# Plain copies out of PSUM for the first chunk's transposed blocks, and a new order of the work, in an adaLN block with sliding-window attention and a gated MLP

## The chip, the cores and the metric

The kernel runs on one core of one Trainium2 chip. The metric is the time of one execution on the device in microseconds (us), lower is better. A kernel's time is the median of its runs; a profile is one execution, with a time of its own. Engines are named as the profile names them: PE is TensorE's matmuls and PEld its weight loads, DVE VectorE, ACT ScalarE, POOL GpSimd, SP SyncE, which issues nearly all transfers.

## What is computed

The input x has one batch of 2048 rows of 640 columns in bf16. A vector c of 640 gives, through w_mod, six rows of 640: shift, scale and gate for the attention (sa, ca, ga) and for the MLP (sb, cb, gb). Both halves normalise x without learned weights, modulate it, and add their gated result.

```python
def _A_ref(x, wqkv, wo):                    # 32 heads of 20, window 256
    q, k, v = ...                           # x @ wqkv
    scores = jnp.einsum('bhqd,bhkd->bhqk', q, k) * Dh ** (-0.5)
    mask = (idx[:, None] - idx[None, :] >= 0) & (idx[:, None] - idx[None, :] < W)
    p = _softmax(jnp.where(mask[None, None], scores, -1000000000.0), axis=-1)
    o = jnp.einsum('bhqk,bhkd->bhqd', p, v)
    return o.transpose(0, 2, 1, 3).reshape(B, S, D) @ wo
...
mod = (_silu(c) @ w_mod)                    # sa, ca, ga, sb, cb, gb
h = _layernorm(x, axis=-1) * (1 + ca) + sa
x = x + ga * _A_ref(h, A_wqkv, A_wo)
h = _layernorm(x, axis=-1) * (1 + cb) + sb
x = x + gb * ((_sigmoid(h @ w_gate) * (h @ w_up)) @ w_down)
```

## The kernel before

**Tiling.** The 2048 rows are cut into eight chunks of 256 rows, each of two blocks of 128. The functions record operations, 2126 in all, for eight chunks that overlap in time: while chunk a is in its attention, chunk a+1 or a+2 is being projected and chunk a−1 is in the MLP.

**A chunk's path.** `ln1` normalises the two blocks of x (statistics on VectorE at L766 and L768, the power −1/2 on GpSimd at L771 and L773, the normalised rows at L786). The result is turned, columns onto partitions, into a tile hT of five blocks (dt 0 to 4) of 128 columns by 256 rows, and modulated with mA, which holds the shift and the scale of the attention. For chunks 0 to 2 TensorE turns it (`pe_transposes`), for later chunks a DMA transpose (L793) does, and `modulate` then works in place in SBUF (L801 on ScalarE, L802 on VectorE or GpSimd). `qkv` multiplies hT with wqkv in pieces of 320 columns (chunk 0) or 480 (the others), and ScalarE (L870) or VectorE (L871) empties PSUM into staging buffers stg, of which there are four, and V. From stg q and k are turned to QT and KT, by TensorE for chunks 0 and 1 and by DMA transposes (L793) for the rest. A score group (matmuls at L680, S<-QT,KT) is followed by exponentials on ScalarE (L981) and masks on GpSimd (L1006); a burst of matmuls multiplies with V (M<-E,V). VectorE turns the result back (T, L1050), divides (L1055, L1057) and turns again (On, L1059); On goes to DRAM and returns as oT. `outproj` multiplies with wo and adds the residual (L1111); the second normalisation and modulation give h2T; `mlp` multiplies with the gate and up weights wg and wu, takes a tanh (L1156) and a product (L1158) to hh, multiplies with wd and adds (L1177).

**The head.** Everything waits for mA: w_mod's first part comes in five slices of 320 KB, and the function fnA adds one group of ten matmuls for each slice; a copy at L752 takes mA out of PSUM. For chunk 0 the five turned blocks lie in PSUM by then, each 128 x 256, and leave it by ten operations of 128 x 128 that modulate on the way (L834 on ScalarE, L835 on VectorE): first the rows of block 0 for all dt, then those of block 1, so that the projection of block 0 can start after five. `mod_rows` makes the other modulation rows in the same manner from the parts of w_mod that are loaded into wu and hh; the scales for wo and wd are multiplied into these weights (L1200, L1139).

**What sets the order.** PRIO, a list at L360, holds one number for each recorded operation: sorting by it gives the order of the program, and the number modulo 5 gives the engine. `schedule` goes through the operations in this order and keeps times of its own estimation, which serve one purpose in the kernel: where a tile has a choice of several buffers, it gets the one that is free earliest by these times. `emit` writes each engine's instructions in that order with the semaphore waits that the data and the buffers need. Thus nothing is reordered on the chip: an instruction that waits holds up all those behind it on its engine, and on SyncE a transfer that waits for its data holds up the transfers behind it. DSAFE (L479) is a time that is added to the estimated end of every load and every DMA transpose (L576, L609, L794). It makes no instruction and no wait; it can change which buffer a tile gets.

Of the kernel before, what the change touches and what calls it, by code (L numbers as in the profile page):

```python
# [7 lines left out]
ACT = mybir.ActivationFunctionType  # L8
# [334 lines left out]
def c_act(n):  # L343
    return 0.17 + n / 1200.0


def c_dve(n, x=1.0):
    return 0.155 + n / 960.0 / x
# [6 lines left out]
def c_pe(n):  # L355
# [117 lines left out]
]  # L473
TR1 = 2
NPH = 3
NPQ = 2
PQ = ()
KEEP = 3
DSAFE = 1.5  # L479
RING = 256  # L480
FETCH = 3.3
START = 0.8
PORTLAG = 0.05
MIXED = 0.39
NPB = 0
# [18 lines left out]
def build(nc, A_x, A_wqkv, A_wo, B_x, B_w_gate, B_w_up, B_w_down, c, w_mod, out, S=2048):  # L504
    NCH = S // CH
    P = Prog(nc)
    A = P.op
# [745 lines left out]
```

## Time and profile before

| | us |
|---|---|
| median of three runs | 328.51 |
| lowest and highest of them | 326.97, 329.53 |
| the profiled execution | 330.57 |
| its span | 328.8 |
| TensorE busy (matmuls) | 320.3 |
| VectorE, ScalarE, GpSimd busy | 211.2, 214.1, 186.3 |
| mean granted clock of TensorE | 0.995 of full speed |

The profiled execution's time is that of the whole launch, 1.77 us longer than the span, which goes from the first instruction in the trace to the last. It lies 2.06 us above the median. The rows of the profile that matter stand in the prediction. In a row of a group the numbers after the bar are busy time, mean ns of one, and the idle time just before it with what ended it; in a row of a timeline they are the start, the length, the engine, the line, the operation, what it writes and reads, the shape and the count, and in brackets the wait.

### The profile page before, as it was taken

What the parts mean: (1) busy time and instruction counts of PE and PEld (TensorE: products, weight loads), DVE (VectorE), ACT (ScalarE), POOL (GpSimd) and SP (SyncE); (2) the same over time, 40 slices, a digit from 0 to 9 for tenths busy, and PEclk for the clock granted to TensorE, in tenths of its full rate; (3) what the DMA queues carried; (4) which work ended last, traced back from release to release, by engine and by line L of the source; (5) the groups of instructions that cost most, each with busy time, mean ns of one, the idle gap of its engine ahead of it and who ended that gap; (6) DMA issues with size and microseconds to landing.
All of it is one profiled execution on the core that took longest, in us unless ns stands there. A gap on an engine that the chain in (4) does not pass through costs nothing.

```text
span 328.8 us, 11616 instructions
## 1 busy us (share of the span) xinstructions
PE 320.3 (97%) x4879; PEld 223.9 (68%) x4879; DVE 211.2 (64%) x419; ACT 214.1 (65%) x317; POOL 186.3 (57%) x273
## 2 busy tenths in 40 slices
PE   8999999989999999999999999999999999999996
PEld 3664545536876568766786567877786778787885
DVE  3689996767599755684576576639463776274242
ACT  2497987868976598888687756886786762112220
POOL 6019769945968586769475848384949392002000
PEclk9999999979999999999999999999999999999999
DMA  7989897999590344932034745330602021302001
GB/s 244 371 287 375 127 238 161 182 226 248 178 166 1 67 117 60 162 62 74 22 70 84 143 72 129 66 87 24 102 3 82 23 57 28 102 20 63 20 22 40
DMA packets 71038, 37.85 MB, mean 115 GB/s; under 512 B 45258, under 2 KB 69066, under 8 KB 70986
## 3 DMA queue, kind: packets, MB, share of 16 engines
q1 hardware_dynamic: 69536, 35.47, 46.8%
q10 hardware_dynamic: 1450, 1.64, 1.9%
q8 instruction: 38, 0.62, 0.8%
q14 instruction: 14, 0.11, 0.2%
HBM read 21.30 MB, written 5.25 MB: 81 GB/s over the span
## 4 chain that ended last, share of the span: by engine, by line
PE 68%; DVE 2%; POOL 1%; issue 0%; ACT 0%; DVEq 0%
PE M L679 58%; PE S L680 6%; PE M L680 5%; POOL E L1006 1%; DVE wd L1139 1%; DVE hh L1158 1%; DVE x L786 0%; DVE hT L802 0%; DVE T L1050 0%; ACT E L981 0%; ACT sig L1156 0%; DVE x L1177 0%; DVEq L328 0%
## 5 line engine op out<-in xcount | busy, mean ns | idle before, releaser
L1006 POOL TENSOR_SCALAR_AFFINE_SELECT E<-E 128x512 bf16<-128x512 bf16 (+1 forms) x176 | 142.9, 836 | 73.0 <-ACT E L981 68.7
L981 ACT ACTIVATE E<-S 128x512 bf16<-128x512 f32 (+2 forms) x184 | 151.0, 879 | 41.7 <-PE S L680 39.6
L679 PE MATMUL M<-wqkv,hT 128*128 128x480 bf16 (+1 forms) x340 | 73.6, 361 | 2.5 <-DMA QT<-stg 1.6
L679 PE MATMUL M<-h2T,wu 128*128 128x256 bf16 x480 | 65.3, 273 | 0.0
L679 PE MATMUL M<-h2T,wg 128*128 128x256 bf16 x480 | 63.8, 273 | 1.0 <-DVE hh L1158 0.6
L1158 DVE SCALAR_TENSOR_TENSOR hh<-sig,M 128x512 bf16<-128x512 f32 x48 | 32.1, 679 | 39.8 <-ACT sig L1156 24.6
L679 PE MATMUL M<-wd,hh 128*128 128x320 bf16 (+2 forms) x396 | 56.9, 296 | 0.7 <-POOL E L1006 0.6
L1156 ACT ACTIVATE sig<-M 128x512 f32<-128x512 f32 x48 | 28.8, 605 | 42.5 <-PE M L679 37.5
L679 PEld LDWEIGHTS M<-wqkv,hT 128*128 128x128 bf16 x340 | 31.1, 99 | 31.0 <-issue 2.4
L679 PEld LDWEIGHTS M<-h2T,wg 128*128 128x128 bf16 x480 | 46.3, 98 | 8.3 <-DVE hh L1158 0.8
L679 PEld LDWEIGHTS M<-h2T,wu 128*128 128x128 bf16 x480 | 44.5, 98 | 7.8 <-issue 0.3
L679 PEld LDWEIGHTS M<-wd,hh 128*128 128x128 bf16 x396 | 37.1, 98 | 15.3 <-POOL E L1006 0.7
L680 PEld LDWEIGHTS S<-QT,KT 20*64 20x64 bf16 (+1 forms) x1856 | 19.9, 101 | 20.1 <-ACT E L981 9.2
L680 PE MATMUL S<-QT,KT 20*64 20x256 bf16 (+5 forms) x1856 | 32.1, 228 | 0.1
L1177 DVE TENSOR_TENSOR x<-M,x 128x320 bf16<-128x320 f32 (+2 forms) x33 | 15.3, 474 | 26.3 <-PE M L679 26.2
L766 DVE BATCH_NORM_STATS2 st<-x 128x6 f32<-128x320 bf16 x64 | 28.3, 478 | 3.0 <-DMA x<-in_A_x_dram 2.5
L1050 DVE STREAM_TRANSPOSE T<-M 128x512 f32<-128x512 f32 x32 | 21.1, 693 | 10.3 <-PE M L680 10.1
L679 PE MATMUL M<-wo,oT 128*128 128x320 bf16 x160 | 24.7, 300 | 0.0
L771 POOL TENSOR_SCALAR st<-st 128x2 f32<-128x2 f32 x16 | 3.6, 228 | 34.8 <-DVE st L768 34.5
L680 PE MATMUL M<-E,V 128*32 128x128 bf16 (+1 forms) x960 | 22.7, 247 | 0.0
L786 DVE TENSOR_SCALAR x<-x,st 128x640 bf16<-128x640 bf16 x26 | 14.1, 566 | 12.6 <-POOL st L773 12.6
L680 PEld LDWEIGHTS M<-E,V 128*32 128x32 bf16 x960 | 19.1, 97 | 4.3 <-issue 1.9
(74 smaller groups left out, 249.9 us busy)
## 6 DMA issues: line engine op xcount, KB each, us to landing
x<-in_A_x_dram SPq DMA_DIRECT2D x23, 160.0 KB
doc<-On SPq DMA_DIRECT2D x64, 40.0 KB
wd<-in_B_w_down_dram SPq DMA_DIRECT2D x4, 480.0 KB
wd<-in_w_mod_dram SPq DMA_DIRECT2D x5, 320.0 KB
wqkv<-in_A_wqkv_dram SPq DMA_DIRECT2D x4, 400.0 KB
wu<-in_w_mod_dram SPq DMA_DIRECT2D x5, 320.0 KB, 4.6
oT<-doc SPq DMA_DIRECT2D x8, 192.0 KB, 3.4
hh<-in_w_mod_dram SPq DMA_DIRECT2D x2, 640.0 KB
```

The lines of the kernel that those rows point to most:

```text
L679: return e.matmul(o, l, r, start=st, stop=sp, skip_group_check=True)
L680: return e.matmul(o, l, r, start=st, stop=sp, tile_position=tp, skip_group_check=True)
L766: A("dve", lambda e, g, bi=bi, j=j: e.bn_stats(v(bi * 12 + j * 6, 6), src[bi].ap[:, j * 320:(j + 1) * 320]), 0.48, reads=[src[bi].r()], wr ...
L771: A("pool", lambda e, g: e.tensor_scalar(v(28, n), var(), EPS, None, op0=ALU.add), 0.2, reads=[st.r(("m", bi)) for bi in range(n)], writes ...
L786: return e.tensor_scalar(dst[bi].ap[:], src[bi].ap[:], v(24 + 2 * bi, 1), v(30 + bi, 1), op0=ALU.subtract, op1=ALU.mult)
L981: A("act", lambda e, eng: e.activation(dst(), src(), ACT.Exp, scale=SM_SCALE), c_act(n), reads=[Sp.r()], writes=[E.r(key)], prio=3, tag=f" ...
L1006: A("pool", lambda e, eng: e.affine_select(rows(dst), rows(src), pattern=[[0, 8], [sign, n]], compare_op=ALU.is_ge, fill=0.0, base=base, c ...
L1050: A("dve", lambda e, g, h=h: e.transpose(T1.ap[:, 512 * h:512 * h + 512], X[h].ap), 0.694, reads=[X[h].r()], writes=[T1.r(h)], prio=3.5, t ...
L1139: A(WSE[1], lambda e, g, t=t: e.tensor_tensor(wd[:, t, :], wd[:, t, :], gbc[:], op=ALU.mult), WS, port=True, reads=[R_wd[t // 3], R_gbc], ...
L1156: A("act", lambda e, g, pg=pg, sg=sg: e.activation(sg.ap[:], pg.ap[:], ACT.Tanh, scale=0.5), c_act(512), reads=[pg.r()], writes=[sg.r()], ...
L1158: A("dve", lambda e, g, pu=pu, sg=sg, f0=f0: e.scalar_tensor_tensor(out=hh.ap[:, f0:f0 + 2, :], in0=sg.ap[:].rearrange("p (a b) -> p a b", ...
L1177: A("dve", lambda e, g, ps=ps, bi=bi, c0=c0, n=n: e.tensor_tensor(x1[bi].ap[:, c0:c0 + n], ps.ap[:, 0:n], x1[bi].ap[:, c0:c0 + n], op=ALU. ...
```

## The change

There are three parts.

1. In chunk 0 the five turned blocks leave PSUM by five plain copies of 128 x 256, which need no mA. `modulate` then works on them in place in SBUF, one operation for each dt, and each waits for the copy of its own dt and for mA. That is ten operations where there were ten. TensorE's transposes for chunks 1 and 2 are as they were.
2. DSAFE goes from 1.5 to 0.3.
3. PRIO is replaced as a whole: both the order and the engine of the 2126 operations. The matmuls are the same ones in another order. Of the five copies four are on ScalarE (dt 1, 0, 3, 4) and one on VectorE (dt 2); of their five modulations four are on VectorE (dt 1, 0, 2, 4) and one on ScalarE (dt 3). In TensorE's order three of the five transposes of chunk 0 come ahead of the last two groups of fnA, where all five came after them. Of the modulations in the MLP's half, 19 are on ScalarE where 12 were, and 11 on GpSimd where 17 were.

```diff
@@ -358,125 +358,125 @@
 PRIO = [
-    153, 158, 283, 203, 1133, 1238, 163, 53, 678, 98, 103, 128, 142, 308, 208, 8, 146, 4, 136, 19, 44, 64, 69, 74, 79,
...
+    138, 143, 233, 128, 653, 33, 1593, 183, 573, 398, 38, 243, 318, 112, 163, 578, 151, 49, 166, 54, 59, 64, 69, 74,
...
-DSAFE = 1.5
+DSAFE = 0.3
@@ -793,14 +793,14 @@
-    def modulate(dst, sc, sh, Rmod, prio, ln, a):
+    def modulate(dst, sc, sh, Rmod, prio, ln, a, turned_by=None):
         for dt in range(NDT):
             def mo(e, g, dt=dt):
                 ap = dst.ap[:, dt, :]
                 if g == "act":
                     return e.activation(ap, ap, ACT.Identity, scale=sc[:, dt:dt + 1], bias=sh[:, dt:dt + 1])
                 return e.tensor_scalar(ap, ap, sc[:, dt:dt + 1], sh[:, dt:dt + 1], op0=ALU.mult, op1=ALU.add)
-            A(MOE, mo, {"dve": 0.34, "act": 0.59, "pool": 0.55}, port=True, reads=[dst.r(("t", bi)) for bi in range(2)] + Rmod,
+            A(MOE, mo, {"dve": 0.34, "act": 0.59, "pool": 0.55}, port=True, reads=[dst.r(k) for k in (turned_by or (lambda dt: (("t", 0), ("t", 1))))(dt)] + Rmod,
@@ -825,15 +825,22 @@
+        if a == 0:
+            for dt, pv, rp in evs:
+                def cp(e, g, dt=dt, pv=pv):
+                    return e.activation(dst.ap[:, dt, :], pv(), ACT.Copy) if g == "act" else e.tensor_copy(dst.ap[:, dt, :], pv())
+                A(("act", "dve"), cp, {"act": c_act(256), "dve": c_dve(256)}, reads=[rp], writes=[dst.r(("t", dt))], prio=1, tag=f"{ln}turn{a}")
+            modulate(dst, sc, sh, Rmod, prio, ln, a, lambda dt: (("t", dt),))
+            return last
         prev = {}
-        for blocks, (dt, pv, rp) in [((bi,), x) for bi in range(2) for x in evs] if a == 0 else [((0, 1), x) for x in evs]:
+        for blocks, (dt, pv, rp) in [((0, 1), x) for x in evs]:
             lo, hi = blocks[0] * 128, blocks[-1] * 128 + 128
...
-            prev[dt] = [A(("act", "dve"), ev, {"act": 0.56, "dve": 0.53} if a else {"act": 0.44, "dve": 0.40}, reads=[rp] + Rmod,
+            prev[dt] = [A(("act", "dve"), ev, {"act": 0.56, "dve": 0.53}, reads=[rp] + Rmod,
```

The numbers in braces are the planner's estimates of durations, in us.

222 rows, old and new, of the table PRIO are left out of this document.

## Prediction

> **What bounds the kernel now.** I read the busy shares first, then the rows of granted clock and of DMA rate over the span's 40 slices (8.22 us each), then what TensorE waited for.
>
> ```profile
> PE 320.3 (97%) x4879; PEld 223.9 (68%) x4879; DVE 211.2 (64%) x419; ACT 214.1 (65%) x317; POOL 186.3 (57%) x273
> ...
> PEclk9999999979999999999999999999999999999999
> ...
> GB/s 244 371 287 375 127 238 161 182 226 248 178 166 1 67 117 60 162 62 74 22 70 84 143 72 129 66 87 24 102 3 82 23 57 28 102 20 63 20 22 40
> ```
>
> TensorE is busy for 97% of the span; the other engines stand near 65%. It idles 328.8 − 320.3 = 8.5 us, so only two things can move the end: that idle time, and the slice in which the clock drops (the ninth, 66 to 74 us). The matmuls themselves are the same before and after.
>
> ```profile
> PE M L679 <- DMA QT<-stg: 1.6, 1, 1.6
> PE S L659 <- DVE E L654: 1.3, 1, 1.3
> PE M L679 <- DVE hT L835: 0.6, 1, 0.6
> PE M L679 <- POOL E L1006: 0.6, 1, 0.6
> PE M L679 <- DVE hh L1158: 0.6, 1, 0.6
> PE M L679 <- DVE T L1050: 0.5, 1, 0.5
> PE M L679 <- ACT hT L801: 0.3, 1, 0.3
> PE M L679 <- DVE V L871: 0.3, 1, 0.3
> ```
>
> The columns are total us, times, longest. 1.3 is the start of the program, which nothing here touches. The largest of the rest is one wait for a staging buffer, and it lies in the slice of the low clock. TensorE's timeline and the windows of that place:
>
> ```profile
> 61.99 1.94 PE L679 MATMUL M<-wo,oT 128*128 128x320 bf16 x13
> ...
> 65.23 0.98 PE L679 MATMUL M<-wqkv,hT 128*128 128x480 bf16 x4 [0.34 <-ACT hT L801]
> 67.81 4.07 PE L679 MATMUL M<-wqkv,hT 128*128 128x480 bf16 x11 [1.59 <-DMA QT<-stg]
> 71.81 0.43 PE L680 MATMUL S<-QT,KT 20*64 20x256 bf16 x24
> ...
> 77.59 2.20 PE L679 MATMUL M<-wqkv,hT 128*128 128x480 bf16 x10
> 79.63 1.25 PE L679 MATMUL M<-h2T,wg 128*128 128x256 bf16 x10
> ```
>
> ```profile
> 68.00:70.00 2.00, 2.00 (x7) 0.85 (x6) 1.93 (x3) 0.32 (x1) 1.82 (x3) 0.54 1.03 245
> 70.00:72.00 2.00, 2.00 (x22) 0.65 (x27) 1.97 (x3) 0.82 (x2) 0.00 (x0) 0.61 0.98 335
> ```
>
> Two waits, 0.34 and 1.59, are followed by 11 matmuls that take 71.81 − 67.81 = 4.00 us, at a granted clock of 0.54 and 0.61 (the column ahead of the last two). Undisturbed, ten of the same shape take 79.63 − 77.59 = 2.04, or 0.204 each: 11 cost 2.24. So the clock took 1.76 more, and the place cost 0.34 + 1.59 + 1.76 = 3.69 us, the largest sum in the span that an order can touch.
>
> **A: the head.** Ten evictions with modulation give way to five copies and five modulations.
>
> ```profile
> 9.88 0.35 PEld L679 LDWEIGHTS S<-silubc,wd 128*128 128x128 bf16 x10 [0.32 <-DMA wd<-in_w_mod_dram]
> ...
> 10.19 0.39 PE L679 MATMUL M<-ident,x 128*128 128x128 bf16 x4
> 10.39 0.17 DVE L752 COPY mA<-S 128x10 f32<-128x10 f32 x1 [1.63 <-PE S L679]
> ...
> 10.67 1.53 DVE L835 TENSOR_SCALAR hT<-M,mA 128x128 bf16<-128x128 f32 x4
> ...
> 11.71 2.20 PE L679 MATMUL M<-wqkv,hT 128*128 128x320 bf16 x15 [0.58 <-DVE hT L835]
> ...
> 15.67 0.23 POOL L771 TENSOR_SCALAR st<-st 128x2 f32<-128x2 f32 x1 [7.44 <-DVE st L768]
> ```
>
> ```profile
> L870 ACT ACTIVATE V<-M 128x160 bf16<-128x160 f32 x4 | 1.2, 309 | 0.1
> ```
>
> ```profile
> L802 DVE TENSOR_SCALAR h2T<-h2T,scB,shB x11: 335/345/794, 78.7 to 302.9; 128x256 bf16<-128x256 bf16 x11
> L802 DVE TENSOR_SCALAR hT<-hT,mA x5: 250/685/822, 42.0 to 145.1; 128x256 bf16<-128x256 bf16 x5
> ```
>
> The modulation's factors mA exist from 10.39 + 0.17 = 10.56; the first projection starts at 11.71, after 0.58 of waiting for the evictions. In the new order three of the five transposes stand ahead of the last two groups of the factors' matmuls, where TensorE waited 0.32 for a slice of w_mod, so their copies (some 0.31 to 0.43 each: the 160-column copy takes 0.309) are done before mA. Then four modulations on VectorE at 0.25 to 0.35 start at 10.56 instead of evictions at 1.53/4 = 0.38 a half block: the first projection matmul can go near 11.3, 0.4 earlier. But the two last transposes still come after mA, and one block (dt 3) takes copy, copy and then 0.6 on ScalarE, to about 12.1, so 0.2 of the wait returns. Taken: **−0.2**, range −0.5 to +0.4. The same VectorE form shows 0.250 at its shortest and 0.822 at its longest; were all four at 0.82, the head would cost 4 × (0.82 − 0.25) = 2.3 us. I take the short end, since GpSimd, the one engine that starts late here, had been idle 7.44 us at 15.67.
>
> The Trainium skill ("SBUF — State Buffer", section "Who interferes with whom") says that VectorE and GpSimd share one pair of SBUF ports as an exclusive lock, so that the later of the two blocks. That speaks against taking modulation from PSUM into SBUF; the spread of 250 to 822 ns agrees with it, and by it the sum would be +2.1 if GpSimd were at work there.
>
> **B: 28 to 41 us.** Two 320 KB slices of w_mod now stand last in the queue of early loads, behind wo, the gate weights and the others; before, they stood in the middle. The matmuls that need them ran at
>
> ```profile
> 32.83 0.86 PE L680 MATMUL M<-wu,silubc 128*32 128x320 bf16 x20
> ```
>
> and are set back by 16 score matmuls, five wide projection matmuls and ten transposes, some 1.9 us: needed near 34.6. The loads run at 375 GB/s in the fourth slice (to 32.9 us) and 127 in the fifth; if all of the fifth's 127 × 8.22 = 1044 KB belonged to them at 375, they would end 2.8 us into it, at 35.7; if little does, at 33. A wait of 0 to 1.1. Taken: **+0.4**, range −0.3 (small waits of this stretch hide behind it) to +1.1.
>
> **C: 64 to 72 us.** Why did the staging buffer come late? SyncE's issues (issue time, its length):
>
> ```profile
> 54.69 0.47 SPq L581 DMA_DIRECT2D wd<-in_B_w_down_dram  x1
> ...
> 62.93 1.25 SPq L793 DMA_TRANSPOSE QT<-stg  x1
> ```
>
> The DMA transpose that empties the buffer is issued at 62.93 and waited for until 67.81, 4.9 us, behind a 480 KB load. In the new order no bulk load stands between the score work of 40 us and the transposes of chunk 3 (that load goes out near 36 us, the next ones behind the transposes), and the PE work between the last write of the buffer and its next use grows from 5.3 to 7.5 us for the transpose waited for, while the other one's falls from 7.8 to 6.5 (counted through both orders at undisturbed durations like those above). Both exceed the 4.9. So the stall goes: **−1.93**. Of the clock's 1.76 I credit half, **−0.9**: the run that was profiled took 330.57, 2.06 over the median, and I can't see that the median run lost the whole of it. Something comes in place of it:
>
> ```profile
> L801 ACT ACTIVATE hT<-hT,mA 128x256 bf16<-128x256 bf16 x15 | 8.7, 601 | 0.0
> ```
>
> ```profile
> 62.16 1.94 ACT L981 ACTIVATE E<-S 128x512 bf16<-128x512 f32 x2 [0.80 <-PE S L680]
> ```
>
> First, four modulations of chunk 4 now follow each other on ScalarE behind two exponentials, 1.94 + 4 × 8.7/15 = 4.3 us after the score group, while TensorE has ten wo matmuls (10 × 1.94/13 = 1.5), five of 0.204, a score group of 0.4 and three matmuls of the first chain (0.6), 3.5 in all, before the last modulated block: **+0.7**. Second, the MLP of chunk 0:
>
> ```profile
> L1050 DVE STREAM_TRANSPOSE T<-M 128x512 f32<-128x512 f32 x32 | 21.1, 693 | 10.3 <-PE M L680 10.1
> ...
> L1059 DVE STREAM_TRANSPOSE On<-Tn 128x1024 bf16<-128x1024 bf16 x16 | 19.8, 1237 | 0.2
> ...
> L871 DVE CAST stg<-M 128x480 bf16<-128x480 f32 x14 | 9.1, 647 | 4.8 <-PE M L679 4.7
> ```
>
> ```profile
> 66.64 0.28 DVE L768 BATCH_NORM_AGGREGATE st<-st 128x2 f32<-128x12 f32 x2
> ...
> 69.92 0.81 DVE L1057 TENSOR_TENSOR Tn<-T,Dr 128x640 bf16<-128x640 f32 x1
> ```
>
> Between the P·V burst of chunk 1 and its first gate matmuls TensorE has 20 wide projections (4.1) and two score groups (0.8), 4.9; VectorE has two T transposes (1.39), an On transpose (1.24), two casts (1.29), aggregation (0.3) and four modulations (1.4), 5.6, with up to 0.8 of a divide left over ahead of them. Gate matmuls take the blocks one by one, which gives 0.4 back. Before, no wait stands at 79.63, because VectorE caught up during the stall. Taken: **+1.1**, range 0.5 to 1.9. Sum of C: −1.93 − 0.9 + 0.7 + 1.1 = **−1.0**, range −3.7 to +0.9.
>
> **D: after 80 us.** The wait of 0.5 for T goes, as the transposes of PSUM are placed ahead of the scaling of wd
>
> ```profile
> L1139 DVE TENSOR_TENSOR wd<-wd,gbc 128x640 bf16<-128x640 bf16 x9 | 6.2, 722 | 0.0
> ```
>
> and the one of 0.6 for GpSimd's mask becomes one of about 0.4 (0 to 1.5), since a residual add now stands behind two such scalings, a divide and an On transpose on VectorE. The 0.6 for hh at the end of the span goes to 0.1, its modulation being on ScalarE. Together −0.5 − 0.2 − 0.5 = −1.2; a wholly new order of some 2,100 operations also makes waits that I can't see one by one, and I put half of it back: **−0.6**, range −1.2 to +2.
>
> **Sum.** −0.2 + 0.4 − 1.0 − 0.6 = −1.4. Against the profiled execution, 330.57 − 1.4 = 329.2; on the scale of the median, 328.51 − 1.4 = **327.1**.
>
> **The rivals.**
>
> *Full recovery (0.20).* The clock comes back whole (−0.9 more), ScalarE and VectorE keep up (−1.8), the late w_mod slices are hidden (−0.4): 324.0, or about 325 with one of them missing. For it: the idle time between operations on ScalarE and VectorE, 35% of the span. Against it: the counts of C.
>
> *Late gate and up weights, slower (0.20).* The second halves of these weights now stand on SyncE behind the stores of On of chunk 1, which wait for VectorE: about 2.9 us after the burst (two T transposes, an On transpose and a little), and the last is the seventh issue, 7 × 0.47 = 3.3 more. Until their first use TensorE has the 4.9 us of above, 64 gate and up matmuls (64 × 1.25/10 less the tails of their groups, some 7.0), two score groups (0.7) and the wait of 1.1: 13.7. So it decides once a landing takes over 13.7 − 6.2 = 7.5 us.
>
> ```profile
> wu<-in_B_w_up_dram SPq DMA_DIRECT2D x2, 384.0 KB, 5.5
> ```
>
> Before it took 5.5, with less ahead of it; 1.5 MB ahead at 375 GB/s add 4.0: 9.5, a wait of 2.0, and a clock loss like that of 68 to 72 us, 1.76, so 327.1 + 3.8 = 330.9, and 332.6 if the clock is lost twice. Against it: 127 to 250 GB/s is all that this stretch moved.
>
> *The clock loss was only in the profiled run (0.12).* Then nothing of it comes back: 327.1 + 0.9 = 328.0. The Trainium skill ("TensorE: Matmul & The Clock Gate", section "What's actually happening") has the clock fall after a free-running idle window of about 3.4 us, differently from run to run, by which the 0.54 here, after 1.93 us of waits, would be a matter of phase.
>
> *The stall stays (0.08).* The other transpose's shorter cover (6.5) fails, and C is worth nothing: about 328.5.
>
> **How the numbers follow.** The forecast has 0.40. One per cent, about what a measurement here can tell from no change, puts the bounds at 325.2 and 331.8. Below 325.2: most of the full recovery and a little of the forecast, 0.21. Above 331.8: half of the late weights, and the forecast's own upper ends (D +2.6, B +0.7, C +1.9 together), 0.23. Between: 0.56. The range takes in the full recovery at 324.0 and the late weights up to 332.2, most of their upper end.
>
> **What would show it.** Right: no wait for QT<-stg, the ninth slice at full clock, a wait for hT near 63 us and one for h2T at the first gate matmuls, a wait for w_mod near 34 us. Wrong: a wait for wg or wu near 80 us, modulations of 0.8 in the head, or a clock below 0.9 anywhere behind a new wait.

## The result and the profile after

| | median us | lowest to highest | executions |
|---|---|---|---|
| before | 327.39 | 326.80 to 329.53 | 20 |
| changed | 329.25 | 327.98 to 330.50 | 20 |

The ratio of changed to before, estimated from all executions and so not exactly the quotient of the two medians, is 1.0047, with a 95% interval of 1.0031 to 1.0063: 0.5% slower, where 0.4% faster was forecast. Yet the profiled execution of the changed kernel took 329.38 us with a span of 327.6, against 330.57 and 328.8 before. So the two profiles say 1.2 us faster and the medians 1.9 us slower. The first lines of the page and all of TensorE's waits in the changed kernel:

```profile
span 327.6 us, 11602 instructions
...
PE 318.1 (97%) x4878; PEld 222.8 (68%) x4879; DVE 216.9 (66%) x420; ACT 216.3 (66%) x322; POOL 184.0 (56%) x267
...
PEclk9999999999999999999999999999999999999999
```

```profile
PE S L659 <- DVE E L654: 1.3, 1, 1.3
PE M L679 <- DVE x L1118: 1.2, 1, 1.2
PE M L679 <- DVE T L1057: 1.1, 1, 1.1
PE S L680 <- issue: 0.8, 1, 0.8
PE M L679 <- DVE h2T L802: 0.7, 1, 0.7
PE M L679 <- DVE hT L802: 0.6, 1, 0.6
PE M L680 <- DVE shB L731: 0.3, 1, 0.3
PE S L679 <- ACT silubc L650: 0.3, 1, 0.3
PE M L680 <- DVE stg L878: 0.3, 1, 0.3
PE M L679 <- ACT hT L801: 0.2, 1, 0.2
PE M L679 <- DVE x L786: 0.2, 1, 0.2
```

The wait for the staging buffer (QT<-stg, 1.6) and the low clock of the ninth slice are gone. In their place stand waits for VectorE: for a residual add (x, 1.2), for the transposes out of PSUM (T, 1.1) and for a modulation of the MLP's input (h2T, 0.7). Where they lie, in TensorE's timeline (line numbers are seven higher than before, behind the new code):

```profile
65.38 3.39 PE L679 MATMUL M<-wqkv,hT 128*128 128x480 bf16 x15 [0.24 <-ACT hT L801]
...
77.53 1.05 PE L679 MATMUL M<-h2T,wg 128*128 128x256 bf16 x8 [0.67 <-DVE h2T L802]
...
91.80 1.49 PE L679 MATMUL M<-h2T,wu 128*128 128x256 bf16 x12 [1.12 <-DVE T L1057]
...
102.14 2.13 PE L679 MATMUL M<-wd,hh 128*128 128x320 bf16 x14 [1.24 <-DVE x L1118]
```

And what VectorE did in the 15 us before the last of them:

```profile
86.07 5.05 DVE L1146 TENSOR_TENSOR wd<-wd,gbc 128x640 bf16<-128x640 bf16 x4
91.04 1.30 DVE L1057 STREAM_TRANSPOSE T<-M 128x512 f32<-128x512 f32 x2
...
95.02 0.43 DVE L1146 TENSOR_TENSOR wd<-wd,gbc 128x640 bf16<-128x640 bf16 x1
...
97.10 1.70 DVE L1146 TENSOR_TENSOR wd<-wd,gbc 128x640 bf16<-128x640 bf16 x2
98.72 1.71 DVE L1064 TENSOR_TENSOR Tn<-T,Dr 128x640 bf16<-128x640 f32 x1
100.46 1.25 DVE L1066 STREAM_TRANSPOSE On<-Tn 128x1024 bf16<-128x1024 bf16 x1
101.63 1.05 DVE L1118 TENSOR_TENSOR x<-M,x 128x320 bf16<-128x320 f32 x2
```

GpSimd meanwhile, with a pause of 4.26 us ahead of the last row:

```profile
85.01 2.56 POOL L1013 TENSOR_SCALAR_AFFINE_SELECT E<-E 128x512 bf16<-128x512 bf16 x3 [0.47 <-ACT E L988]
87.54 3.23 POOL L1146 TENSOR_TENSOR wd<-wd,gbc 128x640 bf16<-128x640 bf16 x2
...
96.51 4.43 POOL L1013 TENSOR_SCALAR_AFFINE_SELECT E<-E 128x1024 bf16<-128x1024 bf16 x4 [4.26 <-ACT E L988]
```

Four scalings of wd take 5.05 us and hold up the two T transposes behind them; a divide of 1.71 and an On transpose of 1.25 hold up the residual adds that TensorE waits for.

### The profile page after: what moved, and what is told of

Read it like the earlier page. It is cut to its first block, busy times and chain, and to the rows that moved or that the text cites. A ratio compares the mean times of both kernels' runs of the same rounds, so it can differ in the third digit from the quotient of the medians.

```text
span 327.6 us, 11602 instructions
## 1 busy us (share of the span) xinstructions
PE 318.1 (97%) x4878; PEld 222.8 (68%) x4879; DVE 216.9 (66%) x420; ACT 216.3 (66%) x322; POOL 184.0 (56%) x267
## 4 chain that ended last, share of the span: by engine, by line
PE 83%; DVE 9%; issue 3%; ACT 1%; DMA 1%; POOL 1%; ACTq 0%; DVEq 0%
PE M L679 70%; PE S L680 7%; PE M L680 6%; DVE wd L1146 2%; DMA x<-in_A_x_dram 1%; DVE Tn L1064 1%; ACT E L988 1%; DVE stg L878 1%; DVE T L1057 1%; DVE x L786 1%; DVE h2T L802 1%; DVE On L1066 1%; POOL E L1013 1%; DVE st L766 1%; POOL st L773 0%
## 5 line engine op out<-in xcount | busy, mean ns | idle before, releaser
L679 PE MATMUL M<-wqkv,hT 128*128 128x480 bf16 (+1 forms) x340 | 71.5, 355 | 0.9 <-DVE hT L802 0.6
L679 PE MATMUL M<-h2T,wu 128*128 128x256 bf16 x480 | 63.6, 273 | 1.1 <-DVE T L1057 1.1
L679 PEld LDWEIGHTS M<-h2T,wg 128*128 128x128 bf16 x480 | 45.5, 98 | 8.6 <-DVE h2T L802 1.1
```

The costliest lines, as they stand in the source:

```text
L679: return e.matmul(o, l, r, start=st, stop=sp, skip_group_check=True)
```

## The experiments

Two theories stood against each other. **A**: the stall near 66 us of the profile before is not in the ordinary execution of that kernel, so that its end gains nothing, and the new waits are the whole difference. **B**: the stall is always there, and the changed kernel gives back its gain somewhere unseen. The times of all runs, each beside the kernel before on the same chip (the intervals are some 1 us wide on either side, so a single row settles no difference under that):

| run | median us (executions) | lowest to highest | before, same chip | ratio, 95% interval |
|---|---|---|---|---|
| before_again | 327.39 (12) | 326.32 to 330.62 | 328.25 | 0.9988, 0.9950 to 1.0025 |
| before_wd_later | 327.53 (10) | 325.86 to 328.77 | 328.25 | 0.9984, 0.9949 to 1.0020 |
| before_new_head | 327.54 (10) | 327.07 to 329.30 | 328.25 | 0.9994, 0.9961 to 1.0026 |
| after_wd_scaling_early | 327.27 (10) | 326.15 to 328.38 | 328.25 | 0.9980, 0.9949 to 1.0011 |
| after_again | 329.44 (10) | 328.57 to 331.32 | 328.14 | 1.0030, 1.0004 to 1.0057 |
| after_residual_first | 327.55 (10) | 327.05 to 329.15 | 328.14 | 0.9980, 0.9955 to 1.0005 |
| after_three_fixes | 326.06 (9) | 325.80 to 327.61 | 328.14 | 0.9929, 0.9897 to 0.9961 |
| before_more_bulk | 330.89 (10) | 329.82 to 332.02 | 328.14 | 1.0067, 1.0037 to 1.0096 |
| after_five_fixes | 326.08 (10) | 325.62 to 326.31 | 327.86 | 0.9945, 0.9922 to 0.9968 |
| before_new_head_wd_later | 328.03 (12) | 327.23 to 329.44 | 327.86 | 1.0001, 0.9970 to 1.0032 |

To see where time goes when the same matmuls run in another order, I take TensorE's delay: for each kernel the undisturbed distances from one start to the next (for each kind of matmul group its median in the profile before) are added up in its own order, and the sum is subtracted from the start in the profile. Where the delay grows, TensorE loses time; the method is good to some tenths. In us, at places counted in us of TensorE's work:

```
place   before,    before_    after   after_five
        profiled   wd_later           _fixes
 12       1.00       1.36      0.77      0.47
 40       3.31       3.75      3.70      2.53
 60       4.16       4.39      4.42      3.84
 64       8.12       5.30      5.22      4.42
 70       8.38       5.55      5.43      4.63
 80       8.70       5.86      6.51      5.00
 92      10.30       7.48      8.23      6.51
 96      10.40       7.59      9.83      6.63
250      15.91      13.07     15.78     12.33
256      16.77      13.93     15.90     12.44
end      18.95      15.70     18.16     14.89
```

**before_again: how often is the stall there?** The kernel before, unchanged.

> The kernel before, unchanged, in many executions with the clock and span of each. Theory A (the stall for the staging buffer near 66 us and its low clock belong to some executions only): most executions show a clock of 1.000 and a span near 325.6 us, a few show about 0.995 and 328 to 329; a profile without the stall has no wait for QT<-stg over 0.3 us and its TensorE is some 3 us earlier from 70 us on. Theory B (the stall is in every execution, and the change loses elsewhere what it gains there): all executions show about 0.995, and the profile has the wait of 1.6 us and the windows of 68 to 72 us near 0.55 to 0.6.

Its profile, by chance, has the stall without the low clock. TensorE's waits (first line) and timeline:

```profile
PE M L679 <- DMA QT<-stg: 1.8, 1, 1.8
```

```profile
68.00 2.39 PE L679 MATMUL M<-wqkv,hT 128*128 128x480 bf16 x11 [1.83 <-DMA QT<-stg]
```

After a longer wait than the 1.59 of the first profile the eleven matmuls take 2.39 us here, not 4.07. Of the 86 executions of the kernel before that stand beside these runs, 14 show a mean clock of 0.989 to 0.995, and every one of them took 329.65 us or more; the others show 1.000 and lie mostly between 326 and 329, their medians at 327.6 to 328.1. Theory A holds for the clock: it falls in about one execution of six, and the profile to predict from was one of them. How often the wait stands without the low clock, as it does here, the times alone do not show.

**before_wd_later: is it the load?**

```diff
 L581 DMACopy oT<-doc 128x2x256
-L581 DMACopy wd<-in_B_w_down_dram 128x3x640
 L793 DmaTransposeAnt QT<-stg 128x8x128
...
 L793 DmaTransposeAnt KT<-stg 128x8x128
+L581 DMACopy wd<-in_B_w_down_dram 128x3x640
 L793 DmaTransposeAnt hT<-x 128x5x128
```

> The kernel before with one 480 KB load of wd issued behind the DMA transposes of chunk 3 in place of ahead of them. Theory A with that load as the cause of the stall: no execution has the low clock, the median stays within 0.3 us of the kernel before, the slow tail (over 328.3) is gone. Theory B: 2 to 3.5 us faster than before. If the load is not what delays the transposes, the wait for QT<-stg stays in some executions as in the kernel before.

SyncE's issue of KT's transpose in the profile before, then its issues and TensorE's row with the load later:

```profile
60.25 2.56 SPq L793 DMA_TRANSPOSE KT<-stg  x1
```

```profile
59.88 1.25 SPq L793 DMA_TRANSPOSE KT<-stg  x1
61.29 1.23 SPq L793 DMA_TRANSPOSE QT<-stg  x1
...
64.03 0.57 SPq L581 DMA_DIRECT2D wd<-in_B_w_down_dram  x1
```

```profile
65.36 3.50 PE L679 MATMUL M<-wqkv,hT 128*128 128x480 bf16 x15 [0.24 <-ACT hT L801]
```

Fifteen matmuls in one row, no wait for the buffer, no execution above 328.77. The median moves by less than its interval shows: 0.9984, and at the least 0.9949, where the 2.83 us that the prediction booked for the stall and its clock would be 0.9914. Issuing KT's transpose takes 1.25 us where it took 2.56, and QT's, the one waited for, goes out at 61.29 where it went out at 62.93. In the table of delays the stretch 60 to 64 costs 0.91 where it cost 3.96.

**before_more_bulk: the cause enlarged.**

```diff
 L581 DMACopy wd<-in_B_w_down_dram 128x3x640
+L581 DMACopy wg<-in_B_w_gate_dram 128x2x768
+L581 DMACopy wu<-in_B_w_up_dram 128x3x768
 L793 DmaTransposeAnt QT<-stg 128x8x128
```

> The kernel before with the suspected cause enlarged: besides the 480 KB of wd, one load of gate weights and one of up weights (from 384 to 576 KB each) are issued ahead of the last DMA transposes of chunks 2 to 4. If bulk loads ahead of the transposes make the stall, every execution has it: a wait for the staging buffer of 3 to 6 us, the clock below 0.997, the median above 330. If the stall comes from elsewhere (a chance phase of the memory, the clock alone), the share of disturbed executions stays as in the kernel before.

TensorE's timeline, and the windows of the place (the granted clock stands ahead of the last two columns):

```profile
66.35 0.58 PE L679 MATMUL M<-wqkv,hT 128*128 128x480 bf16 x2 [1.57 <-ACT hT L801]
68.25 4.48 PE L679 MATMUL M<-wqkv,hT 128*128 128x480 bf16 x13 [1.31 <-DMA KT<-stg]
```

```profile
68.00:70.00 2.00, 1.75 (x5) 0.57 (x6) 1.37 (x3) 1.09 (x1) 1.73 (x4) 0.58 1.13 250
70.00:72.00 2.00, 2.00 (x7) 0.73 (x6) 1.97 (x3) 0.57 (x1) 1.10 (x1) 0.57 0.72 163
```

All ten executions have the low clock (0.989 to 0.995) and all are above 329.8. The size was missed: the wait for a staging buffer is 1.31 us in this profile, not 3 to 6, and one of 1.57 for hT stands ahead of it. But the cause is shown: with more bulk loads ahead of the DMA transposes the low clock comes in every execution, and with the one load moved behind them (before_wd_later) in none. The changed kernel has no such load there, and its clock is 1.000 in every execution.

**before_new_head: part 1 alone.**

```diff
 L669 Matmult S<-E 128x512
+L679 Matmult M<-ident,x 128x128 x6
 L679 Matmult S<-silubc,wd 128x64 x10
...
+L831 TensorCopy hT<-M 128x256
 L752 TensorCopy mA<-S 128x10
-L835 TensorScalarPtr hT<-M,mA 128x128 x4
+L802 TensorScalarPtr hT<-hT,mA 128x256 x4
```

> The kernel before with part 1 of the change alone: chunk 0's blocks leave PSUM by five plain copies, are modulated in SBUF, and three of the five transposes stand ahead of the last two groups of w_mod, all else in the order of before. If the head gains what it did in the changed kernel's profile, the first projection starts near 11.3 us in place of 11.7, and the time falls by 0.2 to 0.4 us (0.999). If the gain is swallowed by the next wait for weights, no change; if the shared use of SBUF by VectorE and GpSimd costs, the modulations take 0.5 us and more each and the time rises by 0.3 to 1.

```profile
10.44 1.12 DVE L802 TENSOR_SCALAR hT<-hT,mA 128x256 bf16<-128x256 bf16 x4
```

```profile
11.19 2.36 PE L679 MATMUL M<-wqkv,hT 128*128 128x320 bf16 x15 [0.62 <-DVE hT L802]
```

Four modulations take 1.12 us, 0.28 each, and the first projection starts at 11.19 where it started at 11.71. Of the 0.5 us, 0.2 is left in the delay at 12 us of work (0.78 against 1.00), and the time shows no difference: the interval is wider than the gain. This profile also bears on A: the load of wd is in its old place, QT's transpose goes out at 61.20, and TensorE has no wait for a staging buffer. before_new_head_wd_later joins this edit with the later load:

> The kernel before with part 1 (the new head) and with the 480 KB load behind the transposes, the rest of its order kept. The head's gain (0.2 to 0.4 us) and the absence of the stall add up: median 326.7 to 327.2, no execution over 328.8 and none with a clock below 1.000. If the head's gain is lost further on, the median is that of the run with the load alone, relative to the kernel before.

A miss in the median, 328.03 against 327.86 for the kernel before, and in the highest execution, 329.44 where none over 328.8 was expected. The clock is 1.000 in all twelve executions, but in its profile new delays between 70 and 76 us of work take back more than the head gave. Half a microsecond gained at one place need not reach the end.

**after_wd_scaling_early: VectorE's pile.** The gate broadcast for wd stood on SyncE behind stores of the attention's result and five bulk loads:

```profile
73.97 0.30 SPq L581 DMA_DIRECT2D doc<-On  x1
74.31 0.38 SPq L581 DMA_DIRECT2D wg<-in_B_w_gate_dram  x1
...
77.05 0.72 SPq L581 DMA_DIRECT2D gbc<-gate  x1
```

so the scalings came only at 86 us, where VectorE has no time left. The edit, on SyncE and on VectorE:

```diff
 L793 DmaTransposeAnt h2T<-x 128x5x128 x2
+L581 DMACopy gbc<-gate 128x640
 L581 DMACopy wu<-in_B_w_up_dram 128x2x768
...
-L581 DMACopy gbc<-gate 128x640
...
 L1066 StreamTranspose On<-Tn 128x1024
-L1165 TensorScalarPtr hh<-sig,M 128x512 x3
-L1146 TensorTensor wd<-wd,gbc 128x640 x4
-L1057 StreamTranspose T<-M 128x512 x2
+L1146 TensorTensor wd<-wd,gbc 128x640 x3
+L1165 TensorScalarPtr hh<-sig,M 128x512 x2
+L1146 TensorTensor wd<-wd,gbc 128x640 x2
+L1165 TensorScalarPtr hh<-sig,M 128x512
+L1057 StreamTranspose T<-M 128x512 x2
```

> The changed kernel with the broadcast of the MLP's gate issued ahead of the stores of chunk 1's attention (it stood behind four of them and five bulk loads, and landed at 84 us), and five of the scalings of wd moved to VectorE's idle time at 80 to 86 us, ahead of the transposes out of PSUM. If VectorE's pile of work between 86 and 102 us is the main cost of the new order, the waits of 1.1 us for T near 91 us and of 1.2 us for the residual add near 102 us shrink to under 0.4 together, and the time falls by 1.5 to 2.2 us, to that of the kernel before. If other waits of the new order are the cost, it falls by less than 0.5 us. If the bulk loads behind the broadcast come late, a wait for wg or wu appears near 82 us.

The wait for T is gone; that for the residual add, which was expected to shrink with it, stays at 1.2. The delay between 82 and 84 us of work grows by 0.11 in place of 1.41. The median can't be told from that of the kernel before (0.9980, up to 1.0011), where the changed kernel is 0.3 to 0.5% above it. That is a fall of 0.5 to 0.7%, 1.6 to 2.2 us, against 1.3 that this place gives: the first of A's two large new waits is worth at least about what its row says, and the rest is within the intervals.

**after_residual_first.**

```diff
 L1146 TensorTensor wd<-wd,gbc 128x640 x2
-L1064 TensorTensor Tn<-T,Dr 128x32x20
-L1066 StreamTranspose On<-Tn 128x1024
 L1118 TensorTensor x<-M,x 128x320 x2
+L1064 TensorTensor Tn<-T,Dr 128x32x20
+L1066 StreamTranspose On<-Tn 128x1024
```

> The changed kernel with one edit: the first two residual adds of chunk 1 stand on VectorE ahead of the divide (1.7 us) and the On transpose (1.25 us). If that order makes the wait of 1.2 us near 102 us, the wait goes and the time falls by 1.0 to 1.4 us below the changed kernel. If VectorE is simply full there, a wait of the same size comes a little later (statistics, the next T) and the time falls by under 0.4 us.

VectorE and TensorE there:

```profile
98.13 1.07 DVE L1118 TENSOR_TENSOR x<-M,x 128x320 bf16<-128x320 f32 x2
99.12 0.81 DVE L1064 TENSOR_TENSOR Tn<-T,Dr 128x640 bf16<-128x640 f32 x1
```

```profile
100.24 2.89 PE L679 MATMUL M<-wd,hh 128*128 128x320 bf16 x20
```

No wait stands at the row of the wd matmuls any more, and the divide, now behind the adds, takes 0.81 in place of 1.71. The median falls from 329.44 to 327.55 on the same chip, 1.9 us, more than the 1.0 to 1.4 expected. This place gives 1.35 of it (the delay grows by 0.25 between 92 and 96 us of work, against 1.60); in its profile another 0.6 lies ahead of 40 us of work, where the edit changes nothing and the loads of B came earlier.

**after_again**, the changed kernel on that chip:

> The changed kernel, unchanged, on the same chip as the others. Theory A: its executions lie close together, all at a clock of 1.000, around 328.2 to 329.5, and above those executions of the kernel before that have no stall by 1.5 to 2 us; where many executions of the kernel before have the stall, the two medians come together.

As expected by A: all clocks 1.000, median 329.44. It lies 1.3 us above the executions of the kernel before at full clock on this chip (median 328.10), a little less than the 1.5 to 2 that were expected. Its profile also has a wait of 1.9 us near 47 us that the first profile lacks:

```profile
44.46 2.54 DVE L1207 TENSOR_TENSOR wo<-wo,gbc 128x640 bf16<-128x640 bf16 x2 [0.69 <-DMA gbc<-gate]
46.92 0.65 DVE L878 CAST stg<-M 128x480 bf16<-128x480 f32 x1
```

VectorE waited 0.69 us for the attention's gate broadcast, which it did not in the first profile, the two scalings of wo behind it took 2.54 us (1.01 there), and a copy that TensorE needs stood behind them.

**after_three_fixes and after_five_fixes: everything found, together.** The first adds to the two edits above one h2T modulation on ScalarE and the two w_mod slices ahead of wo's load:

```diff
 L581 DMACopy x<-in_A_x_dram 128x640
+L581 DMACopy wu<-in_w_mod_dram 128x1280 x2
 L581 DMACopy wo<-in_A_wo_dram 128x5x640
...
-L802 TensorScalarPtr h2T<-h2T,scB,shB 128x256 x4
+L802 TensorScalarPtr h2T<-h2T,scB,shB 128x256 x3
...
-L801 Activation h2T<-h2T,shB,scB 128x256
+L801 Activation h2T<-h2T,shB,scB 128x256 x2
```

> The changed kernel with the gate broadcast and five scalings of wd early, as in the run before; with the first two residual adds of chunk 1 ahead of the divide and the On transpose; with one of chunk 0's h2T modulations on ScalarE in place of VectorE; and with the two w_mod slices ahead of the 800 KB load of wo. Theory A (the new order costs by these four waits and by nothing large besides): the waits for T, for the residual add, for h2T and for w_mod are gone (each under 0.3 us), the span falls from 327.5 to 323 to 324.5, the time to 324.8 to 326.2, 1 to 1.5% below the changed kernel and 0.5 to 1% below the kernel before. Theory B (each wait removed is replaced by the next one): over 327.

326.06: theory A, within its bounds. The waits for T, the residual add and h2T are gone from the profile; a new one of 0.38 for up weights shows at 85.72, so the broadcast ahead of the loads has its price. The wait of 1.9 us near 47 us that after_again showed is in this profile too, behind the late gate broadcast for wo, and the profiled execution, 327.61, is the slowest of the nine. The second:

```diff
 L878 TensorCopy V<-M 128x8x20
+L878 TensorCopy stg<-M 128x24x20
+L723 TensorScalarPtr gq<-M 128x160
+L878 TensorCopy KT<-M 128x4x128
 L1207 TensorTensor wo<-wo,gbc 128x640 x2
...
 L581 DMACopy wu<-in_B_w_up_dram 128x2x768
-L581 DMACopy wd<-in_B_w_down_dram 128x3x640
+L581 DMACopy wu<-in_B_w_up_dram 128x3x768
```

> The changed kernel with the four fixes of the run before and two more, for what that run's profile showed: the first two scalings of wo behind three copies on VectorE, so that a late gate broadcast near 44 us holds up no copy (a wait of 1.9 us in two of five profiles of the new order), and one 576 KB load of up weights ahead of a 480 KB load of wd (it landed at 85.7 us, a wait of 0.4 us). If these two are what is left, no profile has a wait over 0.7 us besides the start, the median falls by 0.3 to 0.8 us below the run before (about 325.5), and no execution is over 326.8. If they are not, the median stays at 326.0 to 326.3.

The median did not fall further (326.08, on another chip), so that part of the expectation missed. What fell is the spread: ten executions within 0.7 us, none above 326.31, as expected. The profile has no wait for stg any more, but against the expectation one over 0.7 is left besides the start:

```profile
PE M L680 <- POOL E L1013: 1.0, 1, 1.0
```

Against the kernel before it is 0.55% faster (0.9945, 0.9922 to 0.9968), and against the changed kernel some 1%: 326.08/329.25 = 0.990, across chips.

## Why the prediction was wrong

**The step that failed** is in part C: "So the stall goes: −1.93. Of the clock's 1.76 I credit half, −0.9." In the profiled execution the stretch from 60 to 64 us of work cost 3.96 us, and in the changed kernel's profile it costs 0.80: against that one execution the stall went as the prediction said. But the two terms were booked against the median, which does not hold the stall: taking it away alone (before_wd_later) left the median at 0.9984, no less than 0.9949. The sum should have started from an execution without it. The hint was on the page: the profiled execution lay 2.06 us above the median, and the prediction used that to halve one of the two terms and leave the other whole. Without the two terms its own remaining sum, −0.2 + 0.4 + 0.7 + 1.1 − 0.6 = +1.4, has the sign of the +1.86 that was measured, and comes near it. That nearness is in part luck: the terms below miss by −0.8 to +1.7 and partly cancel. The base was off too: 328.51 was the median of three executions, and twenty give 327.39. The rival with only the clock missing from the median run (328.0) came nearest in mechanism, and still took the wait out of the median.

**Term by term**, the delay of the changed kernel against that of before_wd_later, the kernel before without its stall (differences of the table's rows; the two end 2.46 us apart):

- A, the head: −0.2 predicted. −0.6 here, −0.2 against the first profile. Right in kind and size.
- The lock on the shared ports, which A weighed from the Trainium skill ("SBUF — State Buffer", section "Who interferes with whom"), did not bite in the head (0.28 us a modulation), as predicted. It bit in D.
- B, the late w_mod slices: +0.4 predicted, +0.5 between 12 and 40 us of work in this profile. The other profiles of the new order without the edit of B lie between −0.2 and +0.2, so this term hangs on when a load lands, as its range said.
- C, hT for chunk 4: +0.7 predicted, −0.1. The same loss is in the undisturbed kernel before (0.24 of wait in both timelines), so there was nothing to add. C, h2T: +1.1 predicted, +0.8 (wait of 0.67). Right in kind and size. The reason given for no such wait before, that VectorE caught up during the stall, is not: the profiles of before_wd_later and before_new_head have no stall, and no wait for h2T either.
- D, T: −0.5 predicted, +0.1. The wait of 0.47 went and one of 1.12 came, on the earlier T, behind the four late scalings. The place was read too narrowly: the prediction looked at the T that waited before.
- D, the mask and the residual add: −0.2 predicted, +1.5. The mechanism was named (a residual add behind two scalings, a divide and an On transpose), the size was not: it counted 0.72 a scaling and 0.81 for the divide, and beside GpSimd's work they took 0.85 (1.70 for two, at 97.10) and 1.71. This is the term furthest off, by 1.7.
- D, hh: −0.5 predicted, −0.7. The rest of the span: +0.6 allowed, about +1.0 (0.5 between 96 and 250, 0.5 behind 256).
- DSAFE has no term in the prediction, and no run here changes it alone: that it costs nothing is not shown.

**The slower rival**, late gate and up weights, was right about the queue and wrong about the cargo. The loads did stand on SyncE behind the stores of On, but what came too late was the small gate broadcast among them, and through it the scalings; no wait for wg or wu appeared in the changed kernel's two profiles.

What the runs leave open: why the new order without its stalls still loses 0.5 us between 96 and 250 us of work; no single wait stands there.

## What to carry to other kernels

Before a stall of a profile is booked as a gain, ask whether the median has it: compare the profiled execution's time with the runs, and its granted clock with theirs. A transfer that is small but starts a chain (a broadcast that many scalings wait for) belongs ahead of bulk loads and of stores that wait for an engine, or its late landing moves a pile of work to where there is no time for it. Durations that are used for a moved VectorE operation have to come from rows with the same company on GpSimd, and even then they depend on which of the two begins first.

## What the runs showed of the hardware

- A low clock is not set by the length of the wait alone. In the first profile 0.34 and 1.59 us of waits within 3 us were followed by eleven matmuls in 4.07 us; in before_again a wait of 0.24 and one of 1.83 were followed by the same eleven in 2.39, at full clock. The traces show what differs. In the first profile the clock stands at half from 68.17 to 71.58 us, for 3.41 us, and the trace's record of full clock ahead of that, from 6.73 us, is 18 times as long. In before_again the record starts at 5.62 us. If both are cut into steps of 3.41 us from there, the stall lies in one step of the first profile and in two of before_again. TensorE's busy time comes first behind the comma, and the granted clock stands ahead of the last two columns:

```profile
64.75:68.17 3.42, 1.49 (x30) 0.53 (x7) 2.72 (x9) 3.22 (x5) 2.79 (x6) 1.00 1.14 146
68.17:71.58 3.41, 3.41 (x10) 1.22 (x8) 3.38 (x4) 1.14 (x2) 1.65 (x2) 0.50 0.99 280
```

```profile
63.64:67.06 3.42, 2.29 (x34) 0.87 (x32) 3.32 (x10) 3.42 (x7) 2.82 (x4) 1.00 1.49 165
67.06:70.47 3.41, 2.48 (x27) 1.16 (x34) 2.78 (x4) 2.04 (x3) 2.67 (x4) 1.00 0.75 163
```

  A step with 1.49 us of work was followed by half clock, steps with 2.29 and 2.48 were not; in before_more_bulk, where the clock falls at 68.31, the step ahead had 0.64, and all ten executions show the low clock. The Trainium skill ("TensorE: Matmul & The Clock Gate", section "What's actually happening") describes a free-running window, by which the phase decides; these runs agree. It names an idle window as the condition, and here a window that was busy for 1.49 of 3.41 us was enough.
- VectorE's operations on SBUF stretch beside GpSimd's. The scaling of wd takes 0.43 us when GpSimd is idle (95.02 us in the changed kernel) and 1.26 on average in the row at 86.07, where GpSimd selects and scales without a pause. It matters which began first: in the changed kernel the divide starts at 98.72, during a mask of GpSimd that runs from 98.42 to 99.75, and takes 1.71; in after_residual_first the divide and a mask start together at 99.12, and the divide takes 0.81. The Trainium skill ("SBUF — State Buffer", section "Who interferes with whom") calls the shared port pair an exclusive lock; the trace agrees, and shows an operation that loses nearly twice its own length to it.
